# Linear attention and two dense layers on one core: weight conversion and the norm's tail in another order

## The chip, the core and the metric

The kernel runs on one core of a Trainium2 chip. The core has TensorE for matmuls, VectorE, ScalarE and GpSimd for elementwise work, and SyncE, whose queue issues every transfer here. Each engine works through a queue of its own; between engines, semaphores make one instruction wait for another. The metric is the time of one execution on the device in microseconds (us), the median of the runs.

## What is computed

The reference, cut to what matters (B = H = 8, S = 576, D = 64, so 4608 tokens of 512; `w_in` 512 x 2048, `w1` and `w2` 512 x 1024, `w3` 1024 x 1024):

```python
kv = einsum('bhsd,bhse->bhde', k, v)
out = einsum('bhsd,bhde->bhse', q, kv)
x = out / sqrt(mean(out * out, -1) + 1e-6) * g_norm      # tokens x 512
h = x @ w_in
g = (a0 + a1*h + a2*h*h + a3*h**3) / (1 + |b0|*|h| + |b1|*h*h + 1e-6)
x = g @ w_out
return ((x @ w1) * (x @ w2)) @ w3 @ w_out2
```

## The kernel before, in words

**Precision.** All matmuls of the two layers are made of three: each operand is split into a high part `hi` (ScalarE, a cast) and a low part `lo` (VectorE, a subtraction), and `mm3` (lines 89 to 92) adds hi x hi, hi x lo and lo x hi. The weights arrive as 64-bit numbers and are turned into 32-bit ones on the core: `to_f32` (lines 146 to 167) takes two instructions of ScalarE and four of VectorE, and the split one more of each (lines 86 and 87). This is called a conversion. A slot is 128 rows of 512 numbers; `wa0` to `wa15` hold `w_in`, `wb0` to `wb15` hold `w_out`, 32 in all. A slot's raw form is loaded by one transfer of 512 KB. A converted tile waits in a list until two more conversions have begun, and is then split (`conv_on`, `DEPTH` = 2).

**Loading phase.** Before the steps, a string of letters (line 444) gives an order of operations: W loads a slot, C converts one, K and Q load a tile of 128 tokens of k and v, or of q; k, t, o, r, n and x are the attention of the first four tiles (kv product, transpose of q, output product with its square, the norm's sums and root, its scaling with the transpose, and the eviction to the layer's input `xh`, `xl`); c loads constants, F splits what is left. It makes the input of block 0, a block being 512 tokens, four tiles.

**Steps.** Then come 144 steps `g`, one for each pair of a block and a slice `m` of 128 of the 2048 hidden numbers; the list `seq` gives the pairs (block 0 with its first 12 slices, blocks 1 to 8, then the last four slices of block 0). A step issues `l1` (12 matmuls into bank `h`, of which there are two), then the elementwise work of three earlier stages, `ew1(g)`, `ew2(g-1)` and `ew3(g-2)`, and `l2(g-3)` (12 matmuls into the four banks `acc0` to `acc3`). The elementwise stages are generators, and `mix` advances them in the order of a string `MIX`: n is `ew1`, s is `ew2`, l is `ew3`, and t, u, v are conversions. `CONV` says how many conversions a step takes in. The string orders what stands in each engine's queue: of the first advance of each generator most is ScalarE's, of the later ones VectorE's.

**Attention in the steps.** The tiles of the next block pass through `q_pe`, `q_out`, `o_pe`, `n_sq`, `n_rms`, `n_rsq`, `n_out`, `x_pe` and `x_out` at set steps and places: place 0 is ahead of `l1`, 1 behind it, 2 and 3 behind `mix`, 4 at the step's end behind `l2`. They share one bank `at` and one tile `at` (lines 301 to 314). `KV_AT` sets at which step a k/v tile is multiplied into the bank `kv`. For block 1 the whole chain from `q_out` to `n_rsq` stands in one step; for later blocks it is spread over four.

**A block's end.** When `l2` has added a block's last slice, `x2_out` (line 494) copies the four banks into tiles `xev` and stores them to DRAM. `xev`, the raw halves `str` of the second layer's weights and their converted tiles `ct` take turns in the four buffers of one tag, `st`; a tile waits until the buffer that it gets has been read, or stored, for the last time. The next block's `l2` begins in the same four banks one step later. From step 28 on, each step also converts a half slot of the second layer's weights in the background (`bg_load`, `bg_conv`), and stores it to DRAM.

**The second layer** (72 steps of 36 matmuls) comes behind, from about 1100 us on.

Of the kernel before, what the change touches and what calls it, by code (L numbers as in the profile page):

```python
# [18 lines left out]
def linear_attention_two_moe_kernel(  # L19
# [281 lines left out]
    def at_tile(shape, i, name):  # L301

        if i < T0:
            tag, bufs = ("xt", T0) if name == "xt" else ("qs", T0 + 2)
            return p0[0].tile(shape, F32, tag=tag, name=name, bufs=bufs)
        return atp.tile(shape, F32, tag="at", name=name)

    def at_ps(i, name):

        if i < T0:  # L310
            tag = {"q": ("acc0", "acc1", "acc2", "acc3"), "o": ("h", "h", "at", "acc0"), "x": ("acc1", "acc2", "acc3", "at")}[name][i]
        else:
            tag = "at"
        return ps_tile(tag, [P, NP, P], 2 if tag == "h" else 1)
# [80 lines left out]
    with tc.manual_schedule():  # L395
# [48 lines left out]
        for op in "WQWCWKWcWkKCCCkKCktWKQktKWWQCkCotQWFooKtroKCWWrrnrnQWnxCWkKCxkKnWWWxkKCx":  # L444
            if op in whole:
                whole[op]()
            else:
                i = count.get(op, 0)
                count[op] = i + 1
                for f in tile_ops[op]:  # L450
                    f(i)
# [43 lines left out]
        def x2_out(j, m):  # L495

            for n in range(KD):
# [3 lines left out]
                else:  # L501
                    t = stp.tile([P, 512], F32, tag="st", name="xev")
                    nc.scalar.copy(t[:, :TA], accs[j][n])
# [53 lines left out]

        def at_step(g, place, f, i):
            todo.setdefault((g, place), []).append((f, i))
# [14 lines left out]
        KV_AT = {0: 8, 2: 9, 5: 10, 8: 11, 10: 12, 13: 13}  # L574
# [8 lines left out]
        for i in range(T0, NTILE):  # L583
            j, t = divmod(i, TPB)
            if j == 1:
                g = 3 * t
                when = ((q_pe, 0, 4), (q_next, 0, 4), (q_out, 1, 0), (o_pe, 1, 1), (n_sq, 1, 2), (n_rms, 1, 3),
                        (n_rsq, 1, 4), (n_out, 2, 0), (x_pe, 2, 1), (x_out, 2, 2))
            else:
                g = base[j - 1] - 1 + 4 * t  # L590
                when = ((q_pe, 0, 4), (q_next, 0, 4), (q_out, 1, 0), (o_pe, 1, 4), (n_sq, 2, 0), (n_rms, 2, 2),
                        (n_rsq, 2, 4), (n_out, 3, 0), (x_pe, 3, 4), (x_out, 4, 0))
            for f, d, place in when:
                at_step(g + d, place, f, i)
# [159 lines left out]
        MIX = "nlstnuntlustustut", "nlstntnltststs"  # L754
        CONV = "1112111211110110110111"
        NG = NBA * MF
        for g in range(NG + SK):
# [17 lines left out]
            if g < NG:  # L775
                l1(g)
                do(g, 1)
                gens["n"] = ew1(g)
            if 0 <= g - 2 < NG:
# [77 lines left out]
```

## Time and profile before

| | |
|---|---|
| median of 3 runs (least, most) | 1744.5 us (1742.09, 1746.83) |
| the profiled execution's own time | 1746.47 us |
| its span | 1744.7 us |
| TensorE matmuls, busy | 1622.0 us (93%) |
| TensorE weight loads, busy | 1300.6 us (75%) |
| VectorE, busy | 1009.7 us (58%) |
| ScalarE, busy | 906.8 us (52%) |
| GpSimd, busy | 202.2 us (12%) |

The span goes from the first to the last instruction of the program; 1.8 us of the profiled execution lie around it. Times in rows are us from the span's start. In rows, PE is TensorE, PEld its weight loads, DVE VectorE, ACT ScalarE, SP SyncE and POOL GpSimd; "q" behind an engine is its queue. "xt<-at,ny" is the tile written and those read; "[0.40 <-DVE xt L374]" says that the engine was idle for 0.40 us before the instruction, and that line 374 on VectorE ended that. The granted clock of TensorE is a share, 1.00 being 2.4 GHz and 0.50 the lower level, 1.2 GHz. Step 0 begins at 60.70 us, step 22 at 258.07, step 28 at 303.83 and step 124 at 948.65, each where `l1` begins.

### The profile page before, as it was taken

The numbers are of one execution on the slowest core, as the hardware profiler recorded it, in microseconds if no ns is written. First come the engines' busy times: TensorE is split into PE (matmuls) and PEld (weight loads), VectorE is DVE, ScalarE is ACT, GpSimd is POOL, SyncE is SP. The second block draws the span as 40 slices with busy tenths as digits, with TensorE's granted clock in tenths as the row PEclk, the third lists the DMA queues.
The fourth block names the chain that finished last, engine by engine and source line by source line (L and its number), as shares of the span: only waits on it lengthen the run. The fifth ranks groups of instructions, "written<-read, shape, count | busy, mean of one in ns | idle before, by whom it ended". The sixth has DMA issues, their size and how long they took to land.

```text
span 1744.7 us, 20087 instructions
## 1 busy us (share of the span) xinstructions
PE 1622.0 (93%) x7232; PEld 1300.6 (75%) x7232; DVE 1009.7 (58%) x1821; ACT 906.8 (52%) x1593; POOL 202.2 (12%) x152
## 2 busy tenths in 40 slices
PE   4686888999999999999999899999999999999999
PEld 4565667777777777777777676888888888888887
DVE  5788687788787877878788897322122222222221
ACT  4576566676777777767777876211112111212121
POOL 0011111121211212212112221000000000000000
PEclk8788999999999999999999999999999999999999
DMA  9732210232323323232221513301010010010000
GB/s 246 219 115 55 84 31 19 85 81 71 102 75 97 79 74 96 74 96 56 75 61 49 184 62 109 133 1 42 8 48 25 24 49 24 25 49 25 24 24 25
DMA packets 173988, 122.96 MB, mean 70 GB/s; under 512 B 118592, under 2 KB 145216, under 8 KB 173376
## 3 DMA queue, kind: packets, MB, share of 16 engines
q1 hardware_dynamic: 173888, 121.67, 24.5%
q8 instruction: 57, 0.93, 0.2%
q14 instruction: 43, 0.35, 0.1%
HBM read 89.13 MB, written 32.51 MB: 70 GB/s over the span
## 4 chain that ended last, share of the span: by engine, by line
PE 58%; DVE 15%; ACT 7%; issue 4%; DMA 2%; SPq 0%; DVEq 0%; ACTq 0%
PE h L90 8%; PE h L92 8%; PE h L91 8%; PE acc L90 6%; PE acc L91 6%; PE acc L92 6%; DVE s L547 3%; ACT n L526 2%; DVE s L543 2%; PE at L91 2%; PE kv L91 2%; PE kv L90 2%; PE at L90 2%; PE at L92 2%; PE kv L92 2%
## 5 line engine op out<-in xcount | busy, mean ns | idle before, releaser
L527 POOL TENSOR_TENSOR s<-s,a 128x512 f32<-128x512 f32 x144 | 200.5, 1392 | 875.0 <-ACT s L525 875.0
L530 DVE TENSOR_TENSOR n<-n,h 128x512 f32<-128x512 f32 x144 | 99.0, 688 | 146.1 <-ACT n L526 146.0
L682 ACT COPY ab<-h 128x512 f32<-128x512 f32 x72 | 42.3, 588 | 265.6 <-PE h L92 265.6
L683 DVE TENSOR_TENSOR ab<-ab,at 128x512 f32<-128x512 f32 x36 | 24.8, 688 | 213.2 <-PE at L92 173.3
L683 DVE TENSOR_TENSOR ab<-ab,kv 128x512 f32<-128x512 f32 x36 | 24.8, 688 | 199.9 <-PE kv L92 199.9
L526 ACT ACTIVATE n<-h,na 128x512 f32<-128x512 f32 x144 | 110.8, 770 | 42.9 <-DVE s L547 42.3
L524 ACT ACTIVATE a<-h 128x512 f32<-128x512 f32 x144 | 85.6, 595 | 83.1 <-PE h L92 82.4
L547 DVE SCALAR_TENSOR_TENSOR s<-n,na,s 128x512 f32<-128x512 f32 x144 | 120.9, 840 | 1.6
L525 ACT ACTIVATE s<-a,ab 128x512 f32<-128x512 f32 x144 | 117.8, 818 | 5.0
L532 DVE SCALAR_TENSOR_TENSOR n<-n,na,h 128x512 f32<-128x512 f32 x144 | 107.2, 745 | 2.3
L540 ACT ACTIVATE y<-s,epsq 128x512 f32<-128x512 f32 x144 | 104.3, 724 | 0.0
L516 DVE TENSOR_TENSOR lo<-s,hi 128x512 fp32r<-128x512 f32 x144 | 98.8, 686 | 3.6 <-ACT hi L514 3.5
L545 DVE SCALAR_TENSOR_TENSOR s<-s,y 128x512 f32<-128x512 f32 x144 | 99.2, 689 | 1.6
L543 DVE SCALAR_TENSOR_TENSOR s<-s,y 128x512 f32<-128x512 f32 x144 | 98.9, 687 | 0.7 <-ACT y L541 0.7
L541 ACT ACTIVATE y<-y 128x512 f32<-128x512 f32 x144 | 91.4, 635 | 4.6
L514 ACT CAST hi<-s 128x512 fp32r<-128x512 f32 x144 | 87.7, 609 | 7.4 <-PE acc L92 5.4
L86 ACT CAST eh<-ab 128x512 fp32r<-128x512 f32 x36 | 22.4, 623 | 106.6 <-DVE ab L683 106.6
L86 ACT CAST el<-ab 128x512 fp32r<-128x512 f32 x36 | 22.4, 623 | 105.5 <-DVE ab L683 105.5
L273 PE MATMUL kv<-vt,kt 128*128 128x128 f32 (+1 forms) x320 | 50.1, 307 | 20.7 <-DMA vt<-in_v_dram 19.7
L381 PE MATMUL at<-ident,xt 128*128 128x128 f32 x132 | 23.6, 307 | 49.0 <-DVE xt L374 49.0
L273 PEld LDWEIGHTS kv<-vt,kt 128*128 128x128 f32 (+1 forms) x320 | 47.0, 218 | 26.5 <-issue 21.9
L363 ACT ACTIVATE ny<-ms 128x8 f32<-128x8 f32 x36 | 7.6, 210 | 107.6 <-DVE ms L357 107.6
(740 smaller groups left out, 4584.3 us busy)
## 6 DMA issues: line engine op xcount, KB each, us to landing
str<-in_moe_w_dram SPq DMA_DIRECT2D x64, 256.0 KB, 3.6
x2d<-xev SPq DMA_DIRECT2D x36, 256.0 KB, 2.1
x<-x2d SPq DMA_DIRECT2D x36, 256.0 KB, 3.4
out_dram<-oev SPq DMA_DIRECT2D x36, 256.0 KB, 2.3
qt<-in_q_dram SPq DMA_DIRECT2D x32, 256.0 KB, 3.3
kt<-in_k_dram SPq DMA_DIRECT2D x32, 256.0 KB, 3.4
vt<-in_v_dram SPq DMA_DIRECT2D x32, 256.0 KB, 4.1
w12d<-ct SPq DMA_DIRECT2D x32, 128.0 KB, 1.8
```

Source lines behind the costliest of these rows:

```text
L90: nc.tensor.matmul(outp, lhsT=lh, rhs=rh, start=first, stop=False)
L91: nc.tensor.matmul(outp, lhsT=lh, rhs=rl, start=False, stop=False)
L92: nc.tensor.matmul(outp, lhsT=ll, rhs=rh, start=False, stop=last)
L525: nc.scalar.activation(out=s, in_=a, func=AF.Identity, scale=ab[:, 1:2], bias=ab[:, 0:1])
L526: nc.scalar.activation(out=n, in_=h, func=AF.Identity, scale=na[:, 3:4], bias=na[:, 2:3])
L527: nc.gpsimd.tensor_tensor(out=s, in0=s, in1=a, op=ALU.mult)
L530: nc.vector.tensor_tensor(out=n, in0=n, in1=h, op=ALU.mult)
L532: nc.vector.scalar_tensor_tensor(out=n, in0=n, scalar=na[:, 1:2], in1=h, op0=ALU.add, op1=ALU.mult)
L540: nc.scalar.activation(out=y, in_=s, func=AF.Abs_reciprocal_sqrt, bias=epsq[:, 0:1])
L543: nc.vector.scalar_tensor_tensor(out=s, in0=s, scalar=EPS_Q, in1=y, op0=ALU.add, op1=ALU.mult)
L545: nc.vector.scalar_tensor_tensor(out=s, in0=s, scalar=2.0, in1=y, op0=ALU.subtract, op1=ALU.mult)
L547: nc.vector.scalar_tensor_tensor(out=s, in0=n, scalar=na[:, 0:1], in1=s, op0=ALU.add, op1=ALU.mult)
```

## The change

Four things are altered; line numbers of the changed kernel are larger by up to 13.

1. The string of the loading phase converts 21 of the 32 slots (before, 11) and loads 23; it has seven k/v tiles multiplied ahead of step 0 (before, eight). `CONV` then has 11 conversions in steps 0 to 20, one in every other step (before, 21 in steps 0 to 21, up to two a step).
2. For block 1, attention tiles with an odd number take the bank `kv` and the buffer of the slot `wb15`, those with an even number the bank `at` and the tile `at`, as before. The tiles start at steps 1, 3, 5 and 7 and pass through the four-step schedule of the later blocks. `KV_AT` leaves the bank `kv` free from step 2 to step 11.
3. For all tiles in the steps, `n_rms` stands at place 0, and `n_rsq` and `n_out` form a generator r, which `mix` advances between the others.
4. `x2_out` copies banks 0 and 2 on ScalarE and banks 1 and 3 on VectorE.

VectorE's queue at its start, before; `wa0r` is the raw first slot, `na` and `gneg` are made of the constants:

```order
L154 TENSOR_SCALAR wa0r<-wa0r 128x512
L158 SCALAR_TENSOR_TENSOR wa0r<-wa0r 128x512
L162 TENSOR_SCALAR wa0r<-wa0r 128x512
L167 TENSOR_TENSOR ct<-wa0r,ct 128x512
L217 TENSOR_SCALAR na<-co_a 128x4
L219 TENSOR_SCALAR gneg<-gcol 128x1
L154 TENSOR_SCALAR wa1r<-wa1r 128x512
```

And now:

```order
L217 TENSOR_SCALAR na<-co_a 128x4
L219 TENSOR_SCALAR gneg<-gcol 128x1
L154 TENSOR_SCALAR wa0r<-wa0r 128x512
L158 SCALAR_TENSOR_TENSOR wa0r<-wa0r 128x512
L162 TENSOR_SCALAR wa0r<-wa0r 128x512
L167 TENSOR_TENSOR ct<-wa0r,ct 128x512
L154 TENSOR_SCALAR wa1r<-wa1r 128x512
```

The constants stand ahead of the first conversion.

VectorE's queue in steps 61 and 62, before, from the last elementwise instruction of step 61; `ms` are the norm's sums, `ny` the root, `xt` the scaled tile, `n`, `s` and `lo` belong to the elementwise stages:

```order
L547 SCALAR_TENSOR_TENSOR s<-n,na,s 128x512
L356 TENSOR_REDUCE ms<-sq 128x8
L357 TENSOR_SCALAR ms<-ms 128x8
L371 TENSOR_TENSOR ny_4450<-ms,ny_4450 128x8
L372 SCALAR_TENSOR_TENSOR ny<-ny_4450,ny 128x8
L374 TENSOR_TENSOR xt<-at,ny 128x512
L530 TENSOR_TENSOR n<-n,h 128x512
L532 SCALAR_TENSOR_TENSOR n<-n,na,h 128x512
L516 TENSOR_TENSOR lo<-s,hi 128x512
```

And now, from the head of step 61:

```order
L358 TENSOR_REDUCE ms<-sq 128x8
L359 TENSOR_SCALAR ms<-ms 128x8
L535 TENSOR_TENSOR n<-n,h 128x512
L537 SCALAR_TENSOR_TENSOR n<-n,na,h 128x512
L373 TENSOR_TENSOR ny_4414<-ms,ny_4414 128x8
L374 SCALAR_TENSOR_TENSOR ny<-ny_4414,ny 128x8
L376 TENSOR_TENSOR xt<-at,ny 128x512
L154 TENSOR_SCALAR str<-str 128x256
L521 TENSOR_TENSOR lo<-s,hi 128x512
```

Sums, root and scaling stood together between two steps' work; now the sums stand ahead of step 61's work and the scaling inside it.

ScalarE's queue at the end of a block, step 62, before:

```order
L541 ACTIVATE y<-y 128x512
L503 COPY xev<-acc_3550 128x512
L503 COPY xev<-acc_3551 128x512
L503 COPY xev<-acc_3552 128x512
L503 COPY xev<-acc_3553 128x512
L389 ACTIVATE xh<-at,gneg 128x4x128
```

Now ScalarE has two of the four, and VectorE this:

```order
L552 SCALAR_TENSOR_TENSOR s<-n,na,s 128x512
L506 COPY xev<-acc_3551 128x512
L506 COPY xev<-acc_3553 128x512
L392 SCALAR_TENSOR_TENSOR xl<-at,gneg,xh 128x4x128
L535 TENSOR_TENSOR n<-n,h 128x512
```

The second and fourth copy stand behind step 62's elementwise work and ahead of `xl` and step 63's. At the end of block 0 (step 14) the first, second and fourth `xev` take the same of the four buffers; at the other ends in the steady steps the fourth takes that of the first or the second.

```diff
--- before.py
+++ after.py
@@ -303,6 +303,8 @@
         if i < T0:
             tag, bufs = ("xt", T0) if name == "xt" else ("qs", T0 + 2)
             return p0[0].tile(shape, F32, tag=tag, name=name, bufs=bufs)
+        if i // TPB == 1 and i % 2:
+            return wp.tile(shape, F32, tag=f"wb{MF - 1}", name=name)
         return atp.tile(shape, F32, tag="at", name=name)
 
     def at_ps(i, name):
@@ -310,7 +312,7 @@
         if i < T0:
             tag = {"q": ("acc0", "acc1", "acc2", "acc3"), "o": ("h", "h", "at", "acc0"), "x": ("acc1", "acc2", "acc3", "at")}[name][i]
         else:
-            tag = "at"
+            tag = "kv" if i // TPB == 1 and i % 2 else "at"
         return ps_tile(tag, [P, NP, P], 2 if tag == "h" else 1)
 
 
@@ -441,7 +443,7 @@
             "r": (n_rms, n_rsq), "n": (n_out, x_pe), "x": (x_out,),
         }
         whole = {"W": w_load, "C": w_conv, "F": conv_flush, "c": consts}
-        for op in "WQWCWKWcWkKCCCkKCktWKQktKWWQCkCotQWFooKtroKCWWrrnrnQWnxCWkKCxkKnWWWxkKCx":
+        for op in "WWWcKWCWCKWQCkWCWCKtkWCWCQWCKtkWCWCQWCKtkWCWCQWCtkWCoWCooWCKorrWCrnrWCnnKWCnxxCxxQkkKKF":
             if op in whole:
                 whole[op]()
             else:
@@ -500,7 +502,10 @@
                     nc.vector.tensor_tensor(out=t[:, :TA], in0=t[:, :TA], in1=accs[j][n], op=ALU.add)
                 else:
                     t = stp.tile([P, 512], F32, tag="st", name="xev")
-                    nc.scalar.copy(t[:, :TA], accs[j][n])
+                    if n % 2:
+                        nc.vector.tensor_copy(t[:, :TA], accs[j][n])
+                    else:
+                        nc.scalar.copy(t[:, :TA], accs[j][n])
                 nc.sync.dma_start(out=x2d[n, :, j * TA:(j + 1) * TA], in_=t[:, :TA])
             del accs[j]
 
@@ -555,6 +560,14 @@
 
         todo = {}
 
+        rms = {}
+
+        def n_fin(i):
+
+            n_rsq(i)
+            yield
+            n_out(i)
+
         def at_step(g, place, f, i):
             todo.setdefault((g, place), []).append((f, i))
 
@@ -571,7 +584,7 @@
         def q_next(i):
             load_q(i + 1)
 
-        KV_AT = {0: 8, 2: 9, 5: 10, 8: 11, 10: 12, 13: 13}
+        KV_AT = {0: 7, 1: 8, 11: 9, 12: 10, 13: 11, 14: 12, 15: 13}
         for i in range(14, NTILE):
             KV_AT[4 * i - 39] = i
         for g, i in KV_AT.items():
@@ -582,15 +595,10 @@
         base = {j: HM + (j - 1) * MF for j in range(1, NBA)}
         for i in range(T0, NTILE):
             j, t = divmod(i, TPB)
-            if j == 1:
-                g = 3 * t
-                when = ((q_pe, 0, 4), (q_next, 0, 4), (q_out, 1, 0), (o_pe, 1, 1), (n_sq, 1, 2), (n_rms, 1, 3),
-                        (n_rsq, 1, 4), (n_out, 2, 0), (x_pe, 2, 1), (x_out, 2, 2))
-            else:
-                g = base[j - 1] - 1 + 4 * t
-                when = ((q_pe, 0, 4), (q_next, 0, 4), (q_out, 1, 0), (o_pe, 1, 4), (n_sq, 2, 0), (n_rms, 2, 2),
-                        (n_rsq, 2, 4), (n_out, 3, 0), (x_pe, 3, 4), (x_out, 4, 0))
-            for f, d, place in when:
+            g = 1 + 2 * t if j == 1 else base[j - 1] - 1 + 4 * t
+            rms[g + 2] = i
+            for f, d, place in ((q_pe, 0, 4), (q_next, 0, 4), (q_out, 1, 0), (o_pe, 1, 4), (n_sq, 2, 0), (n_rms, 2, 0),
+                                (x_pe, 3, 4), (x_out, 4, 0)):
                 at_step(g + d, place, f, i)
 
         def x0_load():
@@ -751,8 +759,8 @@
                 if i + 2 < KF2:
                     w3_load(i + 2)
 
-        MIX = "nlstnuntlustustut", "nlstntnltststs"
-        CONV = "1112111211110110110111"
+        MIX = "nrlstunnrtulstustustu", "nrlstnnrtlststst"
+        CONV = "101010101010101010101"
         NG = NBA * MF
         for g in range(NG + SK):
             for m, u in last_use.items():
@@ -776,6 +784,8 @@
                 l1(g)
                 do(g, 1)
                 gens["n"] = ew1(g)
+                if g in rms:
+                    gens["r"] = n_fin(rms[g])
             if 0 <= g - 2 < NG:
                 gens["l"] = ew3(g - 2)
             if 0 <= g - 1 < NG:
```

## Rows read from the trace of the kernel before

**Rows 1.** by stretch: busy us (instructions) of engines, clock, DMA share, GB/s

```profile
0.00:60.70 60.70, 28.80 (x137) 25.81 (x137) 37.81 (x78) 29.77 (x55) 1.63 (x8) 0.80 0.98 220
60.70:84.48 23.78, 16.44 (x78) 12.81 (x78) 14.90 (x29) 13.33 (x24) 4.22 (x3) 0.86 0.90 278
60.70:258.07 197.37, 156.61 (x683) 123.32 (x682) 151.45 (x263) 129.27 (x222) 31.23 (x22) 0.89 0.33 95
258.07:303.83 45.76, 39.83 (x179) 31.90 (x178) 35.30 (x58) 30.24 (x52) 8.91 (x7) 0.93 0.14 30
303.83:948.65 644.82, 617.71 (x2879) 493.10 (x2878) 510.96 (x1012) 483.45 (x868) 127.36 (x96) 0.99 0.29 78
948.65:1744.70 796.05, 779.03 (x3365) 626.44 (x3363) 274.22 (x414) 234.03 (x398) 33.03 (x21) 1.00 0.15 49
...
954.42:960.01 5.59, 5.59 (x26) 4.52 (x24) 4.74 (x11) 4.57 (x9) 1.29 (x2) 1.00 0.09 27
```

**Rows 2.** VectorE alone by short stretch, same view

```profile
16.64:19.56 2.92, 2.75 (x6) 1.00 1.36 218
39.00:39.79 0.79, 0.76 (x4) 0.85 1.30 232
46.50:47.58 1.08, 0.94 (x5) 0.50 0.79 303
58.08:58.74 0.66, 0.66 (x2) 0.50 1.38 223
```

**Rows 3.** timeline of VectorE and SyncE at the start: start, length, instruction

```profile
14.24 0.15 DVE L219 TENSOR_SCALAR gneg<-gcol 128x1 f32<-128x1 f32 x1 [0.99 <-DMA gcol<-in_g_norm_dram]
...
9.85 1.19 SPq L213 DMA_DIRECT2D gcol<-in_g_norm_dram  x2
```

**Rows 4.** DMA queues from 0 to 60 us

```profile
DMA packets 29593, 13.11 MB, mean 219 GB/s; under 512 B 24624, under 2 KB 28951, under 8 KB 29591
```

**Rows 5.** who TensorE waited for, 60.7 to 258.1: total, times, longest

```profile
PE at L381 <- DVE xt L374: 27.2, 5, 9.1
PE acc L90 <- ACT xev L503: 3.7, 3, 1.7
```

**Rows 6.** the same view, 258.1 to 303.8 us

```profile
PE at L381 <- DVE xt L374: 4.4, 1, 4.4
PE acc L91 <- DVE lo L516: 1.4, 1, 1.4
```

**Rows 7.** the same view, 303.8 to 948.6 us

```profile
PE at L381 <- DVE xt L374: 13.4, 18, 1.8
PE acc L90 <- ACT xev L503: 10.8, 11, 2.2
PE at L326 <- DVE xl L390: 1.6, 4, 0.4
```

**Rows 8.** timeline of TensorE, end of step 62 and step 63

```profile
538.37 0.66 PE L381 MATMUL at<-ident,xt 128*128 128x128 f32 x4 [0.40 <-DVE xt L374]
544.20 0.50 PE L90 MATMUL acc<-hi,wb0hl 128*128 128x512 f32 x1 [0.98 <-ACT xev L503]
546.26 0.66 PE L326 MATMUL at<-ident,qt 128*128 128x128 f32 x4 [0.41 <-DVE xl L390]
```

**Rows 9.** timeline of ScalarE, same steps

```profile
536.67 0.21 ACT L363 ACTIVATE ny<-ms 128x8 f32<-128x8 f32 x1 [3.18 <-DVE ms L357]
540.83 1.06 ACT L503 COPY xev<-acc 128x512 f32<-128x512 f32 x2
543.56 1.27 ACT L503 COPY xev<-acc 128x512 f32<-128x512 f32 x2 [1.68 <-DMA x2d<-xev]
```

**Rows 10.** timeline of VectorE, same steps

```profile
542.59 0.75 DVE L547 SCALAR_TENSOR_TENSOR s<-n,na,s 128x512 f32<-128x512 f32 x1
```

**Rows 11.** VectorE's PSUM copies in the second half: ns least, median, most

```profile
L704 DVE COPY oev<-acc x18: 683/691/692, 1218.4 to 1740.8; 128x512 f32<-128x512 f32 x18
```

**Rows 12.** who ScalarE waited for, 303.8 to 948.6 us

```profile
ACT ny L363 <- DVE ms L357: 76.9, 24, 3.3
```

## The prediction

> **What bounds the kernel now.** Read the busy time by stretch first [rows 1]. The span falls into five: the loading phase up to step 0 (60.70 us), steps 0 to 21, in which 21 weight slots are still converted (197.37), steps 22 to 27 (45.76), the steady steps 28 to 123 (644.82), and the rest (796.05, with TensorE busy for 779.03 of it), where the change touches next to nothing. A step with matmuls alone, the stretch from 954.42 to 960.01, takes 5.59 us [rows 1], so 22 steps could pass in 123, and they take 197. Three rows tell why: TensorE is busy for 156.61 of the 197.37, its granted clock was 0.89 on the mean (1 is 2.4 GHz), and VectorE is busy for 151.45. VectorE is near to being the bound there, but it isn't: it idles for 46 us. Then the waits of TensorE: its largest in steps 0 to 21 is the transpose of the normed tile at L381, 27.2 us in only 5 waits, the longest 9.1 [rows 5]; in the steady steps the same wait is 13.4 us in 18, and the second one is for the block-end copies, 10.8 us in 11 [rows 7]. So the norm's chain (square, sum, root, scale, transpose) and the block's end are what holds TensorE, not the sum of any engine's work.
>
> **The change, part by part.** The sum is made against the profiled execution, 1746.47 us with a span of 1744.7; the median of the runs, 1744.5, is 2.0 below it.
>
> *Ten conversions move ahead of step 0.* One conversion with its split takes VectorE 2.92 us (the first of [rows 2]), in ten 29.2. Before, VectorE was busy for 37.81 us ahead of step 0 [rows 1]; the last tile's xl and one lo, 1.4 us, fell just behind that line and now stand ahead of it for one half, so I add 0.7: 67.7 busy. In the rows a busy microsecond of conversion takes 2.92/2.75 = 1.06 of time [rows 2], so 71.8. The other parts of the phase are the same work as before: per tile 0.79 for the sums, 1.08 for the scaling, 0.66 for xl [rows 2]. The constants now stand ahead of the first conversion on VectorE, and gneg waits for gcol. Before, gcol landed 4.4 us after its issue began (9.85 to 14.24) [rows 3]; now it is issued behind three weight loads, by my estimate from the same queue at about 4.5, and VectorE begins at about 9 (before, its first conversion began as soon as the first load was in). 9 + 71.8 is 80.8, and I add 1.2 for waits on Q tiles: step 0 starts at **82**, which is **+21.3**. From below: 79, if no wait shows and the constants land early. From above, the loads: 23 weight slots of 524 KB, 7 pairs of K and V tiles of 524 KB and 4 Q tiles of 262 KB are 16.8 MB, and 219 GB/s [rows 4] moves them in 77 us, just ahead of VectorE. As both are close, each can hold up the other, and I put the upper end at 90. The DMA share of 0.98 in that stretch [rows 1] says that the queues were full at that rate.
>
> The Trainium skill, page "DMA: Bandwidth & Descriptors", section Specifications, gives about 358 GB/s of HBM for a core and says that transfers below 512 B don't reach line rate. By that figure alone the loads would take an estimated 47 us, and the upper end would fall to 82; the row, with most packets under 512 B, has 219, and the row decides.
>
> *Steps 0 to 21.* VectorE's 151.45 lose 29.2 and gain two evictions of 0.69 [rows 11]: 123.6. TensorE's floor: 19 steps of 5.59 and three without the second matmul group at half of that, 114.6, and the attention's matmuls. Those I take from the steady stretch: 617.71/96 = 6.43 busy a step, 0.84 over 5.59, thus 3.4 for a tile's four steps; block 1's four tiles, most of the next three and nine K and V parts come to some 7.4 tiles' worth, 25. The floor is 139, above VectorE's 123.6 and ScalarE's (129.27 less ten conversions), so TensorE becomes the bound. The chain of block 1 that stood inside one step, its 27.2 us of waits [rows 5], is spread over four steps with two tiles in flight on separate banks. What is left above the floor: the first three steps, which fill the pipeline (23.78 with 16.44 busy now [rows 1]; I keep 7 of waits), the end of block 0 (3.7 now [rows 5]; I take 4, since the fourth copy waits for the second's store and the second for the first's, all on one buffer), 2 where a conversion step makes VectorE late, 3 of slow clock. 139 + 16 is **155**, **-42.4**. Bounds: 148, if VectorE is never late; 168, if half of the 58 us between 197.4 and 139 stays.
>
> *Steps 22 to 27.* They wait for 4.4 and 1.4 [rows 6], and the clock was 0.93. No conversion is left in them. 45.76 becomes 39, **-6.8**; the busy time of 39.83 at a full clock would be some 38.
>
> *Steps 28 to 123, the norm's tail.* Before, the sums stood behind a step's order, so ScalarE's root waited for VectorE (3.18 us in the row, which held up the next step's work on ScalarE) and the transpose at the step's end waited for xt, 0.40 [rows 8, 9]. Now the sums stand at a step's head, in VectorE's idle time, and root and scaling inside the order, a step and a half before the transpose. Cover: VectorE is busy for 510.96 of 644.82 [rows 1], and the work is the same. All of the 13.4 goes.
>
> *The evictions.* Before, all four copies stand on ScalarE; the third began at 543.56, after waiting for the first one's store [rows 9]. Two copies on VectorE take 0.69 each instead of about 0.6 [rows 9, 11]. But the second one now stands in VectorE's queue behind the step's elementwise work, which ended at 543.34 in that step (542.59 + 0.75 [rows 10]), where ScalarE had begun it at 541.3. The fourth waits for the second's store, on VectorE, with xl and the next step's work queued behind it. So the stores (540.83 to 543.56 less a copy: 2.1 us) still pace the block's end. In favour: ScalarE reaches its first copy about 1.3 to 1.9 us earlier, since its wait for the root is gone. Bounds for a block's end: 1.8 less (all of 10.8/6 [rows 7]), or 2 more (the second copy late by 2, and the fourth with it). I take 0.4 less, as both move by nearly the same, over six ends -2.5, and the 1.6 for xl [rows 7], which goes with the earlier third copy. Together with the tail: **-17.5**. The rest of the span has one such end and the last: **-0.5**.
>
> Sum: 21.3 - 42.4 - 6.8 - 17.5 - 0.5 = -45.9; 1746.5 - 45.9 = 1700.6, and 2.0 off for the median: **1698.6 us**.
>
> **The rivals.** (1) *Loads and latencies hold the first phase.* Transfers of 16.8 MB and VectorE's work alternate instead of overlapping, step 0 starts at 90 (+8 on my 82), and half of the excess stays in steps 0 to 21 (+13): 1719.6. For it: 0.98 of DMA share, and waits of which only the largest are explained; against it: loads run at least three slots ahead of their conversion. (2) *The steps reach the floor everywhere*, 79 and 148, and the block ends lose all 10.8: 1698.6 - 3 - 7 - 8 = 1680.6. Against it: the stores pace the ends. (3) *Slower: ScalarE's wait for the sums moves into the step's order.* It is 76.9 us over 24 tiles now, 3.2 each [rows 12], at a place where it mostly costs nothing. In the new order the root stands ahead of hi and y, which the next matmul group needs. If VectorE comes to the sums late, each microsecond stands before hi, and so before TensorE. It turns my gain into a loss from 45.9/32 tiles = 1.4 us a tile; at half of the present wait, 1.6 a tile, it is 51 us, the gain of 13.4 is gone too, and the time is 1763. Against it: the sums need only the square, which is ready early in the step, and VectorE's idle time lies just there. (4) *The change doesn't do what it says*: waits in other places eat the gain, and loading gives back what the steps save. The time is then within 0.3% of now, about 1743. It needs the 42.4 to shrink to the 21.3 that loading costs and the steady gain to vanish as well.
>
> **How the numbers follow.** Forecast 0.60 (about 1689 to 1711); (1) 0.20; (2) 0.09; (3) 0.07; (4) 0.04. A difference of 0.3% (5.2 us) is about what a measurement of this kernel can tell from no change. The range reaches over the forecast and (2) to 1682, and over (1) with a little on top to 1724; outside lie (3), (4) and the ends of (1) and (2), under 2 in 10. Faster: 0.89, the same 0.04, slower 0.07.
>
> **What would show it.** Step 0 starts near 82 and step 22 near 237; VectorE is busy nearly without a break from 9 us until step 0. In steps 0 to 21 TensorE's clock is at 0.95 or more, and the wait for xt at the transposes is gone there and in the steady steps. The four steps of a steady group without a block's end sum to 25.1 or less. The block ends still stall by 2 to 5 us, on the second and fourth copy now, released by VectorE. I am wrong if step 0 starts after 90, if steps 4 to 11 take over 7.3 us each, if ScalarE's root waits inside the order and hi comes late by as much, or if the block ends grow.

## The result and the profile after

The changed kernel takes **1705.25 us** (median of 4 runs, 1704.38 to 1707.87); the kernel before, beside it, 1743.34 (1742.09 to 1746.83). The ratio is **0.9781**, with a 95% interval of 0.9762 to 0.9800. Forecast were 1698.6, so 6.7 fewer. The profiled execution took 1707.87 with a span of 1706.1, which is 38.6 below the span before; the sum had 45.9.

The busy time by stretch of the changed kernel, the same five stretches as in [rows 1], each from the first matmul of its first step (columns: stretch, its length, busy time of each engine, granted clock, DMA share, GB/s):

```profile
core 0: us, PE busy (x) PEld busy (x) DVE busy (x) ACT busy (x) POOL busy (x), PEclk, DMA share, GB/s
0.00:81.00 81.00, 29.45 (x129) 26.11 (x129) 65.49 (x129) 48.35 (x87) 1.63 (x8) 0.87 0.82 211
81.00:239.74 158.74, 144.15 (x691) 115.72 (x690) 130.50 (x223) 112.78 (x194) 30.95 (x21) 0.97 0.36 95
239.74:278.38 38.64, 37.41 (x179) 30.30 (x178) 30.75 (x50) 27.96 (x48) 9.41 (x7) 1.00 0.16 35
278.38:908.75 630.37, 613.51 (x2880) 494.99 (x2878) 526.73 (x1024) 475.28 (x856) 125.50 (x96) 0.99 0.29 80
908.75:1706.10 797.35, 778.92 (x3365) 626.64 (x3363) 276.54 (x419) 231.16 (x394) 33.58 (x21) 1.00 0.15 49
```

| stretch | before | forecast | after | off by |
|---|---|---|---|---|
| up to step 0 | 60.70 | +21.3 | 81.00 (+20.3) | -1.0 |
| steps 0 to 21 | 197.37 | -42.4 | 158.74 (-38.6) | +3.8 |
| steps 22 to 27 | 45.76 | -6.8 | 38.64 (-7.1) | -0.3 |
| steps 28 to 123 | 644.82 | -17.5 | 630.37 (-14.5) | +3.0 |
| rest | 796.05 | -0.5 | 797.35 (+1.3) | +1.8 |

What TensorE waits for in steps 0 to 21 (first three rows; us in total, times, longest), where [rows 5] had 27.2 us for `xt`:

```profile
PE kv L273 <- DMA vt<-in_v_dram: 4.4, 1, 4.4
PE acc L90 <- DVE xev L506: 3.1, 2, 1.9
PE acc L91 <- DVE lo L521: 1.9, 3, 1.6
```

And in the steady steps, where [rows 7] had 13.4 for `xt` and 10.8 for the copies:

```profile
PE acc L90 <- DVE xev L506: 9.8, 10, 1.6
PE acc L90 <- ACT xev L508: 5.7, 5, 2.0
PE acc L91 <- DVE lo L521: 0.6, 2, 0.3
```

The transposes' wait for `xt` is gone from both lists, as forecast. A wait for a v tile is new, and the wait for the block-end copies has grown from 10.8 to 15.5 us.

**Step 15** takes 16.60 us (before, 11.18), where steps 13, 14 and 17 take 6.5 to 6.9. SyncE's queue in it (start, duration, transfer):

```profile
185.03 6.23 SPq L509 DMA_DIRECT2D x2d<-xev  x4
191.35 1.31 SPq L248 DMA_DIRECT2D kt<-in_k_dram  x2
192.71 1.30 SPq L248 DMA_DIRECT2D vt<-in_v_dram  x2
```

TensorE's waits in it:

```profile
188.10 0.50 PE L90 MATMUL acc<-hi,wb0hl 128*128 128x512 f32 x1 [1.93 <-DVE xev L506]
190.97 0.50 PE L90 MATMUL acc<-hi,wb0hl 128*128 128x512 f32 x1 [1.20 <-DVE xev L506]
196.30 2.04 PE L273 MATMUL kv<-vt,kt 64*128 64x128 f32 x8 [4.37 <-DMA vt<-in_v_dram]
```

Block 0's four stores each wait for a copy, and SyncE spends 6.23 us on them; the loads of the next k/v tile stand behind them in the same queue, and TensorE waits 4.37 us more for that tile. Afterwards its granted clock is lower for a while: it is 0.92 in step 16, which needs 8.40 us for matmuls that take 7.77 at 1.00 in e2 below.

**The block ends.** What the engines of the copies waited for ahead of them, in the steady steps (us, times):

```profile
  DMA x2d<-xev: 21.2, 10
  DMA w12d<-ct: 5.7, 2
  DVE ct L167: 5.1, 2
  DMA wo2d<-ct: 3.8, 1
  DMA w3d<-ct: 1.9, 1
```

All of it, 37.7 us over six block ends, is waiting for one of the four buffers `st`: for an earlier copy's store (21.2) or for a background conversion that holds one.

### The profile page after: what moved, and what is told of

It is laid out like the page before. It is cut to its first block, busy times and chain, and to the rows that moved or that the text cites. A ratio compares the mean times of both kernels' runs of the same rounds, so it can differ in the third digit from the quotient of the medians.

```text
span 1706.1 us, 20053 instructions
## 1 busy us (share of the span) xinstructions
PE 1603.4 (94%) x7232; PEld 1293.8 (76%) x7232; DVE 1030.0 (60%) x1839; ACT 895.5 (52%) x1575; POOL 201.1 (12%) x152
## 4 chain that ended last, share of the span: by engine, by line
PE 73%; DVE 12%; ACT 6%; DMA 3%; issue 3%; SPq 2%; DVEq 0%; ACTq 0%
PE h L90 10%; PE h L92 10%; PE h L91 10%; PE acc L90 9%; PE acc L91 9%; PE acc L92 9%; PE at L91 2%; PE kv L91 2%; PE kv L90 2%; PE at L90 2%; PE at L92 2%; PE kv L92 2%; PE kv L273 2%; DVE s L552 2%; ACT n L531 2%
## 5 line engine op out<-in xcount | busy, mean ns | idle before, releaser
L552 DVE SCALAR_TENSOR_TENSOR s<-n,na,s 128x512 f32<-128x512 f32 x144 | 123.5, 858 | 1.9
L152 ACT ACTIVATE ct<-ct 128x256 f32<-128x256 int32 (+1 forms) x112 | 53.6, 479 | 3.5
L87 DVE TENSOR_TENSOR el<-ab,el 128x512 fp32r<-128x512 f32 x36 | 24.9, 692 | 24.7 <-ACT el L86 24.7
```

What stands on the lines that cost most here:

```text
L552: nc.vector.scalar_tensor_tensor(out=s, in0=n, scalar=na[:, 0:1], in1=s, op0=ALU.add, op1=ALU.mult)
```

## The experiments

All times are medians of 4 runs (e11: 10), each with the kernel before on the same chip; the differences named are between these medians. First all of them by stretch, so that each can be read against the others; the length of a stretch is from the profiled run. The kernel before had medians of 1743.1 to 1745.4 beside the different sets of runs, so 2 us between two sets say nothing. A stretch differs between profiles too: with the conversions ahead and the same loading string, step 0 came at 79.6 to 81.7 us.

| kernel | to step 0 | 0 to 21 | 22 to 27 | 28 to 123 | rest | median | ratio to before (95%) |
|---|---|---|---|---|---|---|---|
| before | 60.7 | 197.4 | 45.8 | 644.8 | 796.1 | 1743.3 | 1 |
| the change | 81.0 | 158.7 | 38.6 | 630.4 | 797.4 | 1705.3 | 0.9781 (0.9762, 0.9800) |
| e1, copies on ScalarE | 79.6 | 159.9 | 38.7 | 629.1 | 795.4 | 1704.4 | 0.9768 (0.9752, 0.9785) |
| e2, k/v load early | 80.0 | 155.3 | 38.7 | 627.1 | 797.2 | 1700.2 | 0.9746 (0.9729, 0.9762) |
| e3, constants late | 82.9 | 161.7 | 38.7 | 627.8 | 798.7 | 1707.6 | 0.9789 (0.9774, 0.9804) |
| e4, conversions late | 59.0 | 173.8 | 40.0 | 628.4 | 799.0 | 1701.8 | 0.9756 (0.9739, 0.9772) |
| e5, ends cleared | 79.6 | 161.0 | 38.7 | 612.5 | 791.6 | 1685.1 | 0.9664 (0.9643, 0.9685) |
| e6, cleared, ScalarE | 81.7 | 158.3 | 38.7 | 607.0 | 791.9 | 1678.7 | 0.9625 (0.9611, 0.9639) |
| e7, four edits, late | 60.3 | 166.0 | 40.1 | 613.1 | 793.6 | 1672.7 | 0.9592 (0.9577, 0.9606) |
| e8, three edits, early | 80.9 | 153.6 | 38.7 | 614.0 | 793.9 | 1679.2 | 0.9620 (0.9601, 0.9639) |
| e9, tail alone | 59.4 | 183.1 | 40.5 | 627.5 | 793.8 | 1707.8 | 0.9796 (0.9778, 0.9814) |
| e10, as e7 on ScalarE | 57.8 | 162.0 | 41.4 | 607.3 | 790.3 | 1664.0 | 0.9538 (0.9518, 0.9557) |
| e11, conversions alone | 79.9 | 180.5 | 39.0 | 645.5 | 798.8 | 1742.8 | 0.9989 (0.9980, 0.9999) |
| e12, all but the tail | 80.3 | 161.7 | 39.5 | 652.6 | 798.4 | 1734.8 | 0.9951 (0.9934, 0.9967) |

The four parts of the change come first (e9, e11, e4, e12, e1), then the new waits (e2, e5, e6), then the loading phase and the versions put together.

**e9: the norm's tail alone.** The kernel before, with this in blocks 2 to 8, and the generator r and the strings `MIX` of the change:

```diff
+                rms[g + 2] = i
-                when = (..., (n_sq, 2, 0), (n_rms, 2, 2),
-                        (n_rsq, 2, 4), (n_out, 3, 0), (x_pe, 3, 4), (x_out, 4, 0))
+                when = (..., (n_sq, 2, 0), (n_rms, 2, 0),
+                        (x_pe, 3, 4), (x_out, 4, 0))
```

> The kernel before, with only the norm's tail moved inside the steps' orders for blocks 2 to 8 (block 1, its single bank, the conversions, the loading phase and the copies stay as they were). Theory (the tail gives all of the gain in the steady steps, the copies on two engines none): the steady steps 28 to 123 take 629 to 632 instead of 644.8, steps 22 to 27 39 to 42 instead of 45.8, steps 0 to 21 within 4 us of 197.4, and the time is 1720 to 1728, 18 to 24 below the kernel before. Rival (the gain in the steady steps came in part from the copies on two engines): the steady steps take 636 or more, the time is 1732 or later.

It takes 1707.8: the tail alone gives 35.3 of the 38 us. The theory was right about the steady steps and wrong about steps 0 to 21. By stretch (steps 0 to 21, then 28 to 123):

```profile
59.38:242.45 183.07, 152.01 (x683) 121.17 (x682) 147.53 (x265) 129.73 (x223) 37.55 (x22) 0.91 0.37 104
282.91:910.45 627.54, 612.97 (x2880) 493.02 (x2878) 521.11 (x1012) 482.62 (x868) 128.56 (x96) 0.99 0.29 80
```

Steps 0 to 21 fall by 14.3 and steps 22 to 27 by 5.3, with all 21 conversions still in them. Block 2's tiles start in steps 11, 15, 19 and 23 and pass through until step 27: step 15 fell from 11.18 to 6.80 us (while step 14 rose from 8.64 to 10.00), step 18 from 10.88 to 6.87, step 22 from 13.05 to 7.12. Steps 8 and 11, where block 1's chain stands, are shorter by 2.2 to 2.7; I put that down to the string `MIX`, which all steps share, but it was not tried alone.

**e11: the conversions alone.** The kernel before, with the loading string and the string `CONV` of the change, and

```diff
-        KV_AT = {0: 8, 2: 9, 5: 10, 8: 11, 10: 12, 13: 13}
+        KV_AT = {0: 7, 1: 8, 3: 9, 5: 10, 8: 11, 10: 12, 13: 13}
```

Block 1's first tile reads one k/v product a step before its last part is added; every matmul is still made.

> The kernel before, with only the loading phase's new order and the ten conversions moved ahead of step 0 (block 1 in one step per tile on one bank, the norm's tail behind the orders, the copies on ScalarE, as before). Theory (the norm's chain, not VectorE's work, held steps 0 to 21): step 0 at 80 to 82, steps 0 to 21 at 172 to 182, the steady steps unchanged at 644.8, and the time between 1738 and 1748, no gain. Rival (the conversions queued ahead of the norm's operations were what made that chain long): steps 0 to 21 at 165 or less, the time 1730 or earlier.

1742.8, no gain. Its stretches, steps 0 to 21 and 28 to 123:

```profile
79.90:260.36 180.46, 152.09 (x691) 121.56 (x690) 131.68 (x220) 114.04 (x196) 28.41 (x21) 0.91 0.32 83
299.40:944.89 645.49, 616.64 (x2879) 492.26 (x2878) 510.96 (x1012) 482.61 (x868) 127.26 (x96) 0.99 0.29 78
```

What TensorE waits for in steps 0 to 21, the largest:

```profile
PE at L381 <- DVE xt L374: 18.9, 5, 4.9
```

The theory's numbers came true, its reason only in part. VectorE has 20 us less to do in steps 0 to 21, and they are 16.9 shorter, so its load was part of what made them long. TensorE still waits 18.9 us for `xt` there, of 27.2 [rows 5], and the steps stay 21.7 longer than in the changed kernel: that is the part of block 1's chain and of the tail. Loading costs 19.2, steps 0 to 21 give 16.9 back, steps 22 to 27 6.7.

**e4: all but the conversions.** The changed kernel with the earlier loading string and `CONV`, and

```diff
-        KV_AT = {0: 7, 1: 8, 11: 9, 12: 10, 13: 11, 14: 12, 15: 13}
+        KV_AT = {0: 8, 11: 9, 12: 10, 13: 11, 14: 12, 15: 13}
```

> The changed kernel, but with the earlier kernel's order of the loading phase and its 21 conversions inside steps 0 to 21; block 1's tiles spread over two banks, the norm's tail inside the steps and the copies on two engines stay. It separates the conversions moved ahead from the rest. Theory (VectorE is next to the bound in steps 0 to 21 once the norm's chain no longer holds them): step 0 starts at 61 (20 us earlier than in the changed kernel), steps 0 to 21 take 172 to 180 instead of 158.7, with VectorE busy for 150 or more of them, and the time is within 5 us of 1705.3. Rival A (the conversions were what held those steps): steps 0 to 21 take 185 or more, the time is 1712 or later. Rival B (moving the conversions only cost time at the start, and spreading block 1 gave all): steps 0 to 21 take 165 or less and the time is 1692 or earlier.

1701.8, 3.4 below the changed kernel. Steps 0 to 21 and two of TensorE's waits in them:

```profile
59.04:232.88 173.84, 149.37 (x682) 119.24 (x682) 150.55 (x267) 128.98 (x221) 45.23 (x22) 0.93 0.39 109
...
PE acc L91 <- DVE lo L521: 7.6, 5, 2.2
PE kv L273 <- DMA vt<-in_v_dram: 4.3, 1, 4.3
```

With 21 conversions inside, these steps are 15.1 longer, and loading is 22.0 shorter. So of the 38.6 us that the change takes off steps 0 to 21, 23.5 (197.4 to 173.8) need no conversion moved. Moving them gives back 15.1 there and 1.4 in steps 22 to 27, and costs 22.0. That this is a loss rests on e7 and e8 below, since the two medians here differ by 3.4 only and their intervals overlap. Against e9, block 1's spread, here together with the copies on two engines, takes 18.9 us off steps 0 to 13 (127.3 to 108.4) and puts 9.7 on steps 14 to 21 (55.8 to 65.5), the k/v load among them.

**e12: all but the tail.** The changed kernel with the earlier places for `n_rms`, `n_rsq` and `n_out` in blocks 2 to 8 (the diff of e9, backwards; block 1 and the strings stay as changed).

> The changed kernel with the norm's tail of blocks 2 to 8 behind the steps' orders again, as before (block 1 keeps it inside; the conversions ahead, the second bank and the copies on two engines stay). Moved alone, the tail took 35 us off the kernel before. Theory A (the parts remove the same waits in steps 0 to 27, so undoing the tail costs less here): steady steps at 643 to 648, steps 0 to 27 up by 3 to 9 us, time 1722 to 1731. Theory B (the parts add up): 1736 to 1742, steps 0 to 27 up by 16 us or more.

1734.8, between the two. The early steps are theory A's: steps 0 to 27 grow by 3.8 us only, where the tail moved alone saved 19.6, so there the parts remove the same waits. The steady steps are neither's, 652.6, which is 7.7 *above* the kernel before:

```profile
PE at L383 <- DVE xt L376: 14.3, 18, 1.4
PE acc L90 <- DVE xev L506: 11.1, 9, 1.8
PE acc L90 <- ACT xev L508: 7.7, 5, 3.0
```

The wait for `xt` is back at 14.3 (13.4 in [rows 7]), and the copies now cost 18.8, where four copies on ScalarE cost 10.8. The six steps behind block ends are 6.0 longer than before, so the copies on two engines are the likely cause. It isn't shown: e12 also keeps the new string `MIX`, which was not tried alone.

**e1: the copies alone.** The changed kernel with

```diff
-                    if n % 2:
-                        nc.vector.tensor_copy(t[:, :TA], accs[j][n])
-                    else:
-                        nc.scalar.copy(t[:, :TA], accs[j][n])
+                    nc.scalar.copy(t[:, :TA], accs[j][n])
```

> The changed kernel with one edit undone: all four copies of a block's end on ScalarE again. Theory (the stores pace a block's end, so the engine of the copies hardly matters, and on VectorE the copies stand behind the step's elementwise work): within 4 us of the changed kernel's 1705.3, rather below it (1701 to 1705); TensorE still waits for the copies in nearly every block end, 10 to 16 us over the steady steps, now all of it released by ScalarE. Rival (two engines share the copies and help): 8 us or more above it, 1713 or later, with block-end steps of 10 to 13 us.

1704.4, the same as the changed kernel. TensorE's wait in the steady steps is on the other engine and nearly as long:

```profile
PE acc L90 <- ACT xev L505: 12.6, 12, 2.0
```

So this part gave nothing: the copies wait for their buffers, whichever engine makes them (37.7 us in the changed kernel, 21.5 here).

**e2: the k/v load ahead of the stores.** The changed kernel with

```diff
-            at_step(g + 1, 4, load_kv, i + 2)
+            at_step(g + 1, 0 if len(segs(i)) == 1 else 4, load_kv, i + 2)
```

> The changed kernel with the load of a K and V tile issued at the head of a step instead of its end, for tiles with one segment. Theory (in step 15 the tile's load stood behind the four stores of block 0 in SyncE's queue, each of which waits for its copy): the 4.4 us wait for vt in step 15 goes, step 15 falls from 16.6 to about 12, the clock of step 16 comes back, and the time is 4 to 6 us below the changed kernel's 1705.3: 1699 to 1701. Rival (the wait hides another one, for the copies or for lo, that ends as late): step 15 stays above 15.5 us and the time within 2 us of 1705.

1700.2, 5.1 less. Step 15, and the queue of SyncE ahead of it and in it:

```profile
184.36:195.28 10.92, 7.78 (x39) 5.64 (x38) 8.70 (x16) 7.76 (x14) 1.28 (x1) 1.00 0.31 107
...
179.75 0.63 SPq L248 DMA_DIRECT2D vt<-in_v_dram  x1
186.97 6.22 SPq L509 DMA_DIRECT2D x2d<-xev  x4
```

The load is issued 7 us ahead of the stores, step 15 is 10.92 instead of 16.60, and its clock is 1.00. The cause of the v tile's wait is shown. Steps 15 and 16 are 6.3 us shorter and steps 0 to 21 together 3.4; the rest of the 5.1 stands in the steady steps, which are nearly as short in e3 without this edit.

**e5: the block ends cleared.** The changed kernel with

```diff
-        BG_AT = [g for g in range(28, 132) if g % 13 not in (0, 4, 8)][:len(bg)]
+        BG_AT = [g for g in range(28, 132) if g % 16 not in (12, 13, 14)][:len(bg)]
```

No background conversion then runs in the step of the copies or in the two behind it, and none is loaded in that step or the two ahead; all 80 are made in other steps.

> The changed kernel with the background conversions of the second layer's weights (a load, a conversion and a store, which use the same four staging tiles as the copies of a block's end) left out of the last three steps of each block and put into the others, 80 as before. Theory (the copies wait for staging tiles that a background conversion or an earlier store still holds): at the block ends of the steady steps all four copies run without a wait for a store, the steps after them (31, 47, 63, 79, 95, 111) fall from 8.2 to 11.9 us to 6.0 to 7.5, and the time is 12 to 20 us below the changed kernel's 1705.3: 1685 to 1693. Rival (the copies themselves, one after the other behind their engine's other work, or the banks, hold the next block's second matmul group): these steps keep 2 us or more over a plain 6.0, and the time falls by less than 6 us.

1685.1, 20.2 less, as the theory had it. Of the six block ends in the steady steps, here is the one in step 47, in the changed kernel and then in this one:

```profile
401.04:412.90 11.86, 8.66 (x32) 5.73 (x30) 7.82 (x15) 7.05 (x13) 1.29 (x1) 0.82 0.31 106
```

```profile
399.68:406.47 6.79, 6.30 (x31) 4.83 (x30) 6.65 (x12) 6.25 (x11) 1.31 (x2) 1.00 0.39 139
```

No copy in the steady steps waits for a buffer any more. The gain of 17.9 us in the steady steps is more than the 15.5 that TensorE waited for the copies: its waits there fall by 11.1 (to 3.9 and 0.5), and its busy time by 8.4 (613.51 to 605.13), since behind the waits of three block ends the clock had been lower (0.82 in step 47, 1.00 now). Behind step 123, where a seventh end was cleared, the time falls by a further 5.8 (797.4 to 791.6). The Trainium skill, page "Perfetto Trace Analysis", section "Optimization Strategy", says that the same gap recurring on the engine that ought to be full can mean a lack of memory for the next tile; this run agrees, 37.7 us of waiting for buffers went, and 11.1 of TensorE's 15.5 with them.

**e6: the block ends cleared, and all copies on ScalarE.** e5 and the diff of e1.

> The run with cleared block ends, and there all four copies on ScalarE: does the engine of the copies matter once every copy has a free staging tile? Theory (with the tiles free, a copy starts when its engine comes to it; TensorE needs the banks only a step's first matmul group later, about 2.6 us): within 4 us of 1685. Rival A (two engines now halve a serial chain of four copies): 1690 or later, with waits for ScalarE's copies of 8 us or more over the steady steps. Rival B (VectorE's copies stand behind its elementwise work, ScalarE's don't): 1681 or earlier.

1678.7, 6.4 below e5: rival B. In e5's step 47 VectorE makes its two copies behind the step's elementwise work, and TensorE waits 0.49 us for the first of them:

```profile
402.49 0.75 DVE L552 SCALAR_TENSOR_TENSOR s<-n,na,s 128x512 f32<-128x512 f32 x1
403.16 1.28 DVE L506 COPY xev<-acc 128x512 f32<-128x512 f32 x2
```

In e6 ScalarE makes all four in a row, and is done before VectorE began (e6's times are 1.2 us ahead of e5's there):

```profile
399.55 2.03 ACT L505 COPY xev<-acc 128x512 f32<-128x512 f32 x4
```

The steps 31, 47, 63, 79 and 95 then take 6.03 us each, as plain ones do, instead of 6.65 to 6.79.

**e3: the constants later.** The changed kernel with `WWWKWCWCKWQCck...` for `WWWcKWCWCKWQCk...` at the start of the loading string.

> The changed kernel with the constants' loads and VectorE's two constant operations put behind the loading phase's first weight and Q loads instead of ahead of the first conversion. In the changed kernel VectorE's first conversion began at 8.97 us, behind the constants, and step 0 at 81.0. Theory (VectorE's queue sets the loading phase, so an earlier begin is an earlier end): the first conversion begins at 4 to 5 us, step 0 at 76.5 to 78, and the time is 3 to 4.5 us below 1705.3. Rival (the transfers set it: they are as long as before): step 0 at 79.5 or later, VectorE idles by 3 us or more elsewhere ahead of it, and the time is within 2 us of 1705.

1707.6, and step 0 at 82.9, later by 1.9. VectorE's first row, and its longest wait:

```profile
4.66 0.43 DVE L154 TENSOR_SCALAR wa0r<-wa0r 128x512 int32<-128x512 uint32 x1 [4.66 <-DMA wa0r<-in_moe_w_in_dram]
...
18.11 0.17 DVE L217 TENSOR_SCALAR na<-co_a 128x4 f32<-128x4 f32 x1 [5.78 <-DMA co_a<-in_moe_a_dram]
```

It begins 4.3 us earlier and then stands 5.8 and 0.4 us for the constants, whose transfers were now issued behind eleven others instead of three; 6.2 - 4.3 = 1.9. The edit missed its aim, and what had been named as signs of the rival came: step 0 later than 79.5, and VectorE idle for over 3 us in another place. Step 0 is later by as much as VectorE lost, as the theory has it, but it also varies by 2 us without any edit there, so e3 doesn't decide between the two. That an earlier begin without the new wait would gain 4 us was not shown.

**e7, e8, e10: put together.** e7 is e4 with the diffs of e2 and e5, and with block 0's end cleared:

```diff
-            if g == len(CONV) - 1:
+            if g == len(CONV) - 1 or g == HM + SK - 1:
                 conv_flush()
-        CONV = "1112111211110110110111"
+        CONV = "1112111211111100110111"
```

e8 is the same on the changed kernel, with its own `CONV` cleared in the same way (`101010101010110010101`). e10 is e7 with the diff of e1.

> Four edits together: the earlier order of loading and conversions inside the steps (as in the run with late conversions), the K and V load at a step's head, the cleared block ends, and block 0's end cleared too (no conversion in steps 14 and 15, the two pending ones finished before its copies). Theory (each removes a wait of its own): 1701.8 less 20 for the cleared ends, less 4 to 5 for the load, less 2 to 4 for block 0's end: 1672 to 1677, step 15 at 7 to 9 us instead of 14.1, step 0 at 59 to 60. Rival (the waits overlap, and what one edit frees another stage takes back): 1680 or later.

> The same three edits on the changed kernel with its 21 conversions ahead of step 0 as they are: the K and V load at a step's head, the cleared block ends, block 0's end cleared. It asks again, without the waits of the block ends, what the conversions ahead are worth. Theory (moving ten conversions ahead costs about 20.5 us of loading and gives back about 15 to 17 in the steps): 1685 less 5 less 2 to 4, thus 1676 to 1679, 2 to 6 us above the run with late conversions. Rival (late conversions were only better because step 15 was bad in the other): it is equal or lower.

> The four edits together (late conversions, the K and V load at a step's head, all block ends cleared), and all four copies of a block's end on ScalarE. Theory (with staging tiles free, the copies on VectorE still cost 0.7 us at each end and more in two of them, as in the run with cleared ends): 1672.7 less 5 to 7, thus 1666 to 1668; the steps behind block ends at 6.0 us. Rival (in the late form ScalarE is fuller and gives that back in steps 0 to 21): 1671 or later.

e7 takes 1672.7 and e8 1679.2, both on the same chip and with no overlap between their runs, so the conversions ahead cost 6.5 us here (3.4 in e4). e7 is in the range expected of it, e8 just above its range and e10 2 us below. e10 takes **1664.0**, 4.6% below the kernel before and 2.4% below the changed one, and is the best of all. Its stretches from step 0 on:

```profile
57.77:219.72 161.95, 145.83 (x682) 116.45 (x682) 149.27 (x265) 129.90 (x223) 46.73 (x22) 0.96 0.41 117
219.72:261.13 41.41, 39.40 (x179) 31.38 (x178) 32.78 (x56) 29.56 (x51) 8.22 (x7) 0.96 0.15 33
261.13:868.43 607.30, 603.80 (x2879) 492.12 (x2878) 522.40 (x1024) 483.48 (x874) 126.42 (x96) 1.00 0.31 85
```

In the steady steps TensorE is busy for 603.80 of 607.30 us. Steps 0 to 21 hold 21 conversions and are only 3.2 longer than the changed kernel's.

## Why the prediction was right, and where it was wrong

All five stretches came out within 4 us of the forecast. What stands behind the numbers was not all as written.

**Loading: right.** VectorE began at 8.97 (forecast 9), was busy for 65.49 (67.7), and step 0 came at 81.0 (82). The transfers moved 211 GB/s at a share of 0.82, where they had been at 0.98 [rows 1], and VectorE waited for the constants (8.7 us) and for ScalarE (2.9), never for a weight slot. So the transfers weren't what set the end, and the first rival's 90 didn't come.

**Steps 0 to 21: the size nearly right, the credit wrong.** The step that failed is the one that gave the conversions and block 1's spread all of the 42.4 and the tail nothing there. The 27.2 us of [rows 5] were written down as block 1's chain. In the trace of before, four of these five waits stand in steps 2, 5, 8 and 11 (23.4 us) and one, 3.8, in step 18, which is a tile of block 2; and e9 shows that the tail alone, with its order of `MIX`, takes 14.3 off the stretch. e11 and e4 show that the conversions ahead are worth 16.9 and 15.1 there, less than loading loses by them (19.2 and 22.0). They were costed as one sum with the spread, and so the question whether they pay for themselves was not asked. VectorE's busy time fell to 130.50 and not to 123.6, as the ten conversions were 20 us of it (e4 has 150.55) and not 29.2; TensorE, busy for 144.15, was the bound all the same.

**Block 0's end: the term that was mis-sized.** I allowed 4 us for it. Steps 15 and 16 took 25.0 us, 9.5 more than their matmuls need at full clock (15.5 in e10); e2 took 6.3 off the two, by the k/v load alone. The load stood behind stores that wait for copies. I had named what queues behind a waiting copy on VectorE, and not what queues behind a waiting store on SyncE, though the change had moved the k/v tiles to just these steps. Without this wait, in e2, the stretch is 155.3, and the forecast was 155.

**Steps 22 to 27: right**, 38.64 for 39, with the reason half right: e9 with conversions still there reaches 40.5, e11 without the tail 39.0. Either of the two removes nearly all of it.

**The steady steps: the tail too small, the copies of the wrong sign.** Tail and `xl` were given 15.0; alone the tail takes 17.3 (e9), and 4.7 of that is TensorE's busy time (617.71 to 612.97), which the sum had left as it was. Of the 18 groups of four steps without a block's end, 11 take 25.1 or less, as forecast, and seven 25.5 to 27.8. The copies were given 2.5; without them the steady steps are 1.3 shorter (e1), too little to tell from nothing, and 5.5 shorter with the buffers free (e5 and e6), and the wait for them grew from 10.8 to 15.5. The prediction had the cause in hand, "the stores still pace the block's end", and yet took a small gain, because ScalarE reaches its first copy earlier. In the trace that first copy then waits for a background tile instead, as in step 47 for 2.56 us:

```profile
405.39 0.58 ACT L508 COPY xev<-acc 128x512 f32<-128x512 f32 x1 [2.56 <-DVE ct L167]
```

Clearing the ends gave 17.9 (e5), and 23.4 with ScalarE's copies (e6). The bound of "all of 10.8" was too small also for the clock: behind the waits in steps 47, 79 and 95 the matmuls were slow as well.

**The rivals.** ScalarE's wait for the sums didn't move into the order: among ScalarE's waits in the steady steps there is none for `ms`, and in steps 0 to 21 there are five, of 5.7 us together. Two of the signs of being wrong did show. Steps 4 to 11 took 7.4 us each on the mean, just over the 7.3 named, by step 10's 9.8 alone. And the block ends grew a little: the six steps behind them took 60.4 us in all, where they had taken 58.8. That the net sum came so near is in part luck: within one sum, the tail was underrated and the conversions were overrated.

## What to carry to other kernels

Cost each part of a change by itself, also when they meet in one stretch: here one part made nearly all of the gain, one made none, and one cost some. When an engine waits at the same place in every round, look at what holds the buffer that the next instruction needs, before its work is given to another engine; changing which steps the background work runs in gave 20 us, the second engine nothing. And a load issued from an in-order queue belongs ahead of stores that wait for something, not behind them.

## What the runs showed of the hardware

A wait of TensorE can cost more than its length, and need not. In step 47 of the changed kernel it waits for copies three times, for 3.2 us in all. The granted clock is 1.00 until 408.6 us, behind the second of these waits, and at its lower level, 0.50, from there into step 48:

```profile
401.04:408.60 7.56, 4.71 (x21) 3.12 (x19) 4.96 (x10) 2.81 (x7) 0.00 (x0) 1.00 0.14 53
408.65:415.40 6.75, 6.40 (x17) 4.63 (x17) 5.37 (x11) 5.58 (x11) 1.29 (x1) 0.50 0.69 195
```

Over the step that is 0.82, and the matmuls take 8.66 us; without the waits, in e5, the clock is 1.00 and they take 6.30. In step 111 TensorE waits for 3.3 us, and the clock stays at 1.00:

```profile
823.92:834.01 10.09, 6.80 (x32) 4.67 (x30) 7.31 (x12) 7.29 (x12) 1.28 (x1) 1.00 0.42 131
```

Of the six steps behind block ends the clock was lower in 47, 79 and 95 (0.82, 0.88 and 0.85), and 1.00 in 31, 63 and 111.

VectorE's `s` at L552 takes 0.75 us, and in some steps up to 1.8. In e5, VectorE's row and GpSimd's at that time:

```profile
806.06 1.81 DVE L552 SCALAR_TENSOR_TENSOR s<-n,na,s 128x512 f32<-128x512 f32 x1
```

```profile
806.03 1.29 POOL L532 TENSOR_TENSOR s<-s,a 128x512 f32<-128x512 f32 x1 [4.31 <-ACT s L530]
```

GpSimd's multiplication began 0.03 us earlier, and VectorE's instruction, which reads two tiles from SBUF, took 1.06 longer than usual. Of the 144 such instructions in e5, 17 took 1.66 to 1.83 us, and each of them had begun 0.01 to 0.38 us behind one of GpSimd's; the other 127 took 0.74 to 0.75, also those during which one of GpSimd's began. Step 111, behind the row shown, is the longest of e5's block ends (8.64 us); that the one made the other was not tried. The Trainium skill, page "SBUF — State Buffer", section "SBUF: two separate sides", says that such an instruction of VectorE and one of GpSimd share a pair of ports, which the one that starts first holds until its end; these rows agree.

Issuing a transfer took SyncE 0.43 to 0.51 us at the start of the loading phase, and up to 3.43 us while many were under way (e3, at 9.30). This is how the constants, behind eleven transfers, came to be issued at 13.33 us.
